# Second weight sums on GpSimd, gate store buffers moved, and alternating output banks in the last score phase of an attention and gate kernel

## The chip, the cores and the metric

One core of one Trainium2 chip. The metric is the device time of one execution in microseconds (us), as the median of a kernel's runs. Before: 920.76 us, median of 3 runs (919.71 to 922.02). "Span" is the profiled execution from its first to its last instruction; it is about 1.8 us shorter than the time of the same run.

## The reference, cut to what matters

```python
# x [1, 2048, 640]; k_cache, v_cache [1, 32, 2048, 192]; wq [640, 6144]; wo [6144, 640]
# w_gate, w_up [640, 1536]; w_down [1536, 640]; all bf16
def _A_ref(x, k_cache, v_cache, wq, wo):          # attention over the last W = 512 keys, 32 heads of 192
    q = (x @ wq) by heads
    k, v = k_cache[:, :, Sk - W:, :], v_cache[:, :, Sk - W:, :]
    p = softmax(q @ k^T * Dh ** -0.5)
    return (p @ v) by rows @ wo
def _B_ref(x, w_gate, w_up, w_down):              # gate
    return (sigmoid(x @ w_gate) * (x @ w_up)) @ w_down
# ... (setup, layernorm, silu)
xn = layernorm(x)
return x + _A_ref(xn, ...) * silu(_B_ref(xn, ...))
```

## The kernel before: the parts that matter

First comes the gate part: four stages of gate and up products, each followed by a down projection (D in the tables is the last of them). Then attention runs over 8 groups of 4 heads, each group twice (once per half of the rows), so 16 runs of a score phase (S) and an attention phase (V). The queries of the next run are worked out between the score groups, and the output products of the run before between the attention groups. The last run differs: its score phase carries the output products of run 15, and after its attention phase comes a tail with its own output products.

The query products use sums and differences of halves of the weights, so each group of heads needs a "raw" load of weights, a scaling to fp16 and a handful of sums in each of 5 chunks:

```python
    def scale_k(key):
        nc.gpsimd.tensor_scalar(k_of[key][:], k_of[key][:], w_down, None, op0=ALU.mult)
    # ...
    def scale_w(g, c):
        raw = raw_t[g, c][:]
        nc.scalar.activation(raw.bitcast(F16), raw, AF.Copy, scale=w_up)
        for k, r in enumerate((LO, HI)):
            nc.scalar.activation(sums_w(g, c, r, 0), part_w(g, c, r, k, 0), AF.Copy)

    def sum_w(g, c):
        a, tt = slice(0, P), nc.vector.tensor_tensor
        TA, TB, TC = (sums_w(g, c, a, i) for i in range(1, 4))
        tt(TB, part_w(g, c, a, 1, 1), part_w(g, c, a, 0, 1), ALU.subtract)
        tt(TA, TB, part_w(g, c, a, 0, 0), ALU.add)
        nc.scalar.activation(sums_w(g, c, HI, 2), part_w(g, c, HI, 1, 1), AF.Copy)
        tt(TC, part_w(g, c, a, 1, 0), TA, ALU.subtract)
        tt(sums_w(g, c, HI, 1), part_w(g, c, HI, 0, 1), part_w(g, c, HI, 0, 0), ALU.subtract)
```

Scores have 64 contract rows, output products have 128. An attention group ends in a transpose by DMA out of one of two output buffers:

```python
    def stage_s(r, i, pp, c, k):
        b0 = 4 + 2 * (k % 2)
        ps = ps_all[:, b0:b0 + 2, :]
        for j in range(PC):
            for b, h in enumerate((LO, HI)):                 # LO, HI: rows 0-63, 64-127
                nc.tensor.matmul(ps[:, b, :], lhsT=kT[h, ...], rhs=qT_t[r][i, j][h, pp, :], ...)
        nc.scalar.activation(E_t[r, i, pp][:, c, :, :], ps, AF.Exp, scale=scale_qk)

    def stage_pv(r, i, pp, h):
        # ... 16 matmuls, then
        nc.vector.tensor_tensor(o_st[...], o_ps[...], rden[...], ALU.mult)
        if h == 1:
            nc.sync.dma_start_transpose(oT[:], o_st[:].rearrange("p q d -> p (q d)"))
```

The first queries, and the loop over runs:

```python
    nc.scalar.activation(mx, w_up, AF.Exp, scale=0.0)        # brings the table for exponentials
    slots = query_slots(0, True, (2, 3), (4, 5), (6, 7, 0))
    for n, k in enumerate((0, 1, 7, 2, 3, 8, 4, 5, 9, 6, 10)):
        slots[k]()
        if n == 1:
            scale_w(1, 0)
        elif n == 3:
            sum_w(1, 0)
            load_raw(1, 3, nc.gpsimd)
    # ...
        for k, x in enumerate(s_list):
            stage_s(r, *x, k)
            # ... queries of the next run; in runs 0 and 1 more scale_w and sum_w
            if r == last and k % 2 == 1:
                ring[:] = [0, 1]
                stage_wo(*wo_list[k // 2])                   # one output tile: always banks 0 and 1
```

The softmax here doesn't subtract the row's maximum and nothing guards it: scores larger than these inputs give would overflow.

## Time and profile before

| what | before |
|---|---|
| median of runs | 920.76 us |
| span of the profiled run | 919.7 us |
| TensorE busy | 896.2 us, 97% |
| VectorE, ScalarE, GpSimd busy | 653.5, 446.1, 220.3 us |
| TensorE not busy | 23.5 us |

How to read it: TensorE is the bound, so a microsecond off another engine is worth nothing unless TensorE waited for it. The 23.5 us without work are the reserve that these shares show (time at a lowered clock counts as busy and comes on top), and they sit in a few stages. So the view that decides is the length of each stage beside the same stage in the steady stretch, and the waits of TensorE name who releases it there. These lines are in the prediction below.

### The profile page before, as it was taken

What the parts mean: (1) busy time and instruction counts of PE and PEld (TensorE: products, weight loads), DVE (VectorE), ACT (ScalarE), POOL (GpSimd) and SP (SyncE); (2) the same over time, 40 slices, a digit from 0 to 9 for tenths busy, and PEclk for the clock granted to TensorE, in tenths of its full rate; (3) what the DMA queues carried; (4) which work ended last, traced back from release to release, by engine and by line L of the source; (5) the groups of instructions that cost most, each with busy time, mean ns of one, the idle gap of its engine ahead of it and who ended that gap; (6) DMA issues with size and microseconds to landing.
All of it is one profiled execution on the core that took longest, in us unless ns stands there. A gap on an engine that the chain in (4) does not pass through costs nothing.

```text
span 919.7 us, 18431 instructions
## 1 busy us (share of the span) xinstructions
PE 896.2 (97%) x7706; PEld 533.6 (58%) x7785; DVE 653.5 (71%) x1089; ACT 446.1 (49%) x528; POOL 220.3 (24%) x201
## 2 busy tenths in 40 slices
PE   9999998898999999999999999999999999999987
PEld 5545454446665656666666666666666566666555
DVE  4879947568667866786678667866786678666556
ACT  4323346586428542854285428542764375424240
POOL 0052135203200320032003201320132011202962
PEclk9999999999999999999999999999999999999999
DMA  9993374407261826192617261727183624265625
GB/s 286 259 264 93 90 152 88 122 19 121 52 122 11 188 53 122 24 175 53 120 30 170 52 121 35 164 53 121 39 161 53 121 45 104 52 105 164 159 80 123
DMA packets 186612, 100.37 MB, mean 109 GB/s; under 512 B 153312, under 2 KB 178912, under 8 KB 186528
## 3 DMA queue, kind: packets, MB, share of 16 engines
q1 hardware_dynamic: 157632, 57.85, 31.4%
q0 software_dynamic: 9408, 29.93, 13.3%
q10 hardware_dynamic: 19488, 11.41, 5.5%
q8 instruction: 61, 1.00, 0.5%
q14 instruction: 23, 0.19, 0.1%
HBM read 57.87 MB, written 5.24 MB: 69 GB/s over the span
## 4 chain that ended last, share of the span: by engine, by line
PE 87%; DVE 4%; ACT 4%; DMA 3%; issue 2%; POOL 0%; SPq 0%; DVEq 0%; POOLq 0%; ACTq 0%
PE ps_all L680 21%; PE ps_all L537 19%; PE ps_all L637 17%; PE ps_all L623 16%; PE ps_all L430 8%; PE ps_all L480 4%; ACT raw L218 1%; ACT E L627 1%; DVE ps_all L694 1%; DVE o_sb L695 1%; PE ps_all L344 1%; ACT sig_sb L435 1%; DMA gB_d<-gB_sb 1%; DVE wB L225 1%; DMA oT<-o_st 1%
## 5 line engine op out<-in xcount | busy, mean ns | idle before, releaser
L627 ACT ACTIVATE E<-ps_all 128x1024 bf16<-128x1024 f32 x256 | 253.3, 1022 | 295.4 <-PE ps_all L623 224.3
L680 PE MATMUL ps_all<-wo_g,oT 128*128 128x128 bf16 (+2 forms) x1474 | 225.1, 296 | 6.4 <-DVE o_sb L695 3.1
L623 PE MATMUL ps_all<-qT,kT 64*128 64x512 bf16 x1536 | 195.3, 376 | 1.9 <-ACT E L627 1.0
L637 PE MATMUL ps_all<-v_sb,E 128*128 128x193 bf16 x2048 | 189.5, 247 | 0.1
L637 PEld LDWEIGHTS <-E 128*128 128x128 bf16 x2048 | 168.7, 98 | 18.2 <-issue 6.4
L680 PEld LDWEIGHTS <-oT 128*128 128x128 bf16 x1536 | 121.6, 98 | 82.6 <-issue 6.4
L571 DVE TENSOR_TENSOR qT<-ps_all,qp 128x512 bf16<-128x512 f32 x176 | 116.9, 688 | 51.8 <-PE ps_all L537 41.7
L558 DVE COPY qp<-ps_all 128x512 f32<-128x512 f32 x150 | 100.8, 688 | 57.8 <-PE ps_all L537 57.7
L623 PEld LDWEIGHTS <-kT 64*128 64x128 bf16 x1536 | 76.4, 94 | 90.8 <-issue 9.0
L644 DVE TENSOR_TENSOR o_st<-ps_all,rden 128x768 bf16<-128x768 f32 x128 | 122.5, 957 | 6.6 <-DMA oT<-o_st 2.0
L202 POOL DMA_DIRECT2D raw<-in_A_wq_dram x80 | 47.9, 604 | 316.5 <-ACT wB L227 235.8
L135 POOL DMA_DIRECT2D k_sb<-in_A_k_cache_dram x32 | 33.4, 1044 | 184.2 <-DMA kT<-k_sb 117.8
L142 POOL TENSOR_SCALAR k_sb<-k_sb,w_sc 128x1536 bf16<-128x1536 bf16 x16 | 67.1, 4193 | 22.2 <-DMA k_sb<-in_A_k_cache_dram 21.9
L218 ACT ACTIVATE raw<-raw,w_sc 128x1536 f16<-128x1536 bf16 x40 | 63.0, 1575 | 1.1
L480 PE MATMUL ps_all<-wd_sb,hT_sb 128*128 128x128 bf16 (+1 forms) x377 | 54.2, 303 | 2.7 <-DVE hT_sb L436 2.3
L714 DVE TENSOR_TENSOR acc<-ps_all,acc 128x640 f32<-128x640 f32 x48 | 39.6, 825 | 22.2 <-PE ps_all L680 22.2
L537 PE MATMUL ps_all<-XA,wA 64*128 64x512 f16 x420 | 52.3, 376 | 2.0 <-DVE qT L571 2.0
L643 DVE RECIPROCAL rden<-ps_all 128x4 f32<-128x4 f32 x128 | 23.2, 181 | 42.5 <-PE ps_all L637 41.2
L537 PE MATMUL ps_all<-XB,wB 64*128 64x512 f16 x420 | 52.7, 376 | 0.4 <-ACT qp L556 0.4
L537 PE MATMUL ps_all<-X,w 64*128 64x512 bf16 x420 | 52.0, 376 | 0.7 <-DVE o_st L644 0.7
L436 DVE TENSOR_TENSOR hT_sb<-ps_all,sig_sb 128x512 bf16<-128x512 f32 x48 | 32.6, 683 | 25.5 <-ACT sig_sb L435 14.8
L435 ACT ACTIVATE sig_sb<-ps_all 128x512 bf16<-128x512 f32 x48 | 28.1, 596 | 40.2 <-PE ps_all L430 37.1
(114 smaller groups left out, 768.3 us busy)
## 6 DMA issues: line engine op xcount, KB each, us to landing
raw<-in_A_wq_dram POOLq DMA_DIRECT2D x80, 192.0 KB, 3.9
k_sb<-in_A_k_cache_dram POOLq DMA_DIRECT2D x32, 192.0 KB, 4.6
wo_g<-in_A_wo_dram ACTq DMA_DIRECT2D x6, 960.0 KB, 6.8
v_sb<-in_A_v_cache_dram ACTq DMA_DIRECT2D x28, 192.0 KB, 3.8
gB_d<-gB_sb POOLq DMA_DIRECT2D x16, 160.0 KB, 2.9
gBa_sb<-gB_d SPq DMA_DIRECT2D x16, 160.0 KB, 3.8
xa_sb<-in_A_x_dram SPq DMA_DIRECT2D x16, 160.0 KB, 3.8
out_dram<-o_sb SPq DMA_DIRECT2D x15, 160.0 KB, 1.8
```

The lines of the kernel that those rows point to most:

```text
L142: nc.gpsimd.tensor_scalar(k_of[key][:], k_of[key][:], w_down, None, op0=ALU.mult)
L218: nc.scalar.activation(raw.bitcast(F16), raw, AF.Copy, scale=w_up)
L430: nc.tensor.matmul(gu[:, i, :], lhsT=w[:, c, f * P:(f + 1) * P], rhs=xnT[s][:, c, :], start=(c == 0), stop=(c == NCD - 1),)
L480: nc.tensor.matmul(oB_ps[:, d0:d0 + dsz], lhsT=hT_sb[:, f, q * P:(q + 1) * P], rhs=wd_sb[:, f, d0:d0 + dsz], start=(f == 0), stop=(f == NF ...
L537: nc.tensor.matmul(ps_all[:, b, :], lhsT=w(r, c), rhs=x[r, c, :], start=(first and k == 0), stop=(k == len(cs) - 1), skip_group_check=True,)
L558: nc.vector.tensor_copy(dst, part(b))
L571: nc.vector.tensor_tensor(q_out(i, u, pp), part(b), t[:], ALU.add)
L623: nc.tensor.matmul(ps[:, b, :], lhsT=kT[h, c * PC + j, :], rhs=qT_t[r][i, j][h, pp, :], start=(j == 0), stop=(j == PC - 1),)
L627: nc.scalar.activation(E_t[r, i, pp][:, c, :, :], ps, AF.Exp, scale=scale_qk)
L637: nc.tensor.matmul(o_ps[:, q // 2, q % 2, 0:DH + 1], lhsT=E[:, c, h, q * P:(q + 1) * P], rhs=vt[:, c, 0:DH + 1], start=(c == 0), stop=(c = ...
L644: nc.vector.tensor_tensor(o_st[:, :, h * DH:(h + 1) * DH].rearrange("p (b i) d -> p b i d", b=2), o_ps[:, :, :, 0:DH], rden[:].to_broadcas ...
L680: nc.tensor.matmul(oA[:, d0 - base:d0 - base + dsz], lhsT=oT_t[r, i, pp][:, q * PC + j, :], rhs=wo_t[runs[r][1]][:, cc, d0:d0 + dsz], star ...
```

## The change

Its intent: (1) take ScalarE and VectorE work out of the last gate stage and the first two runs by giving the second group's weight sums to GpSimd; (2) lay the buffers of the gate stores where the first queries don't write; (3) keep GpSimd's key scaling from colliding with VectorE, by moving it to VectorE; (4) give the output tiles of the last score phase two bank groups in turn; (5) cut the last output tile into three pieces.

```diff
     def scale_k(key):
-        nc.gpsimd.tensor_scalar(k_of[key][:], k_of[key][:], w_down, None, op0=ALU.mult)
+        nc.vector.tensor_scalar(k_of[key][:], k_of[key][:], w_down, None, op0=ALU.mult)
... (scale_w is split into scale_raw and copy_w; sum_w takes its engine as an argument)
+    def second_w(c):
+        copy_w(1, c, nc.gpsimd.tensor_copy)
+        sum_w(1, c, nc.gpsimd.tensor_tensor, nc.gpsimd.tensor_copy)
+        load_raw(1 + (c + 3) // NCD, (c + 3) % NCD, nc.gpsimd)
 
     with ExitStack() as bctx:
+        gpool = bctx.enter_context(tc.tile_pool(name="gpool", bufs=4))
         wB = bctx.enter_context(tc.tile_pool(name="wB", bufs=1))
         bwork = bctx.enter_context(tc.tile_pool(name="bwork", bufs=2))
-        gpool = bctx.enter_context(tc.tile_pool(name="gpool", bufs=4))
...
-                    for c in {0: (0,), 2: (1,), 5: (2,), 7: (3,), 10: (4,)}.get(f, ()):
+                    for c in {0: (0,), 2: (1,), 5: (2,), 8: (3,)}.get(f, ()):
                         scale_w(0, c)
-                    for c in {1: (0,), 3: (1,), 6: (2,), 8: (3,), 11: (4,)}.get(f, ()):
+                    for c in {1: (0,), 3: (1,), 6: (2,), 9: (3,)}.get(f, ()):
                         sum_w(0, c)
...
-                if s == 3 and q in (1, 2):
-                    sum_x(pi, 3 + q, sw)
-                elif s == 3 and q == 3:
-                    load_k((1, 0))
+                if s == 3:
+                    if q == 0:
+                        scale_w(0, NCD - 1)
+                    else:
+                        scale_raw(1, q - 1)
+                    if q == 1:
+                        sum_w(0, NCD - 1)
+                        load_raw(1, 2, nc.gpsimd)
+                    if q < 3:
+                        sum_x(pi, 3 + q, sw)
+                    else:
+                        load_k((1, 0))
...
         if r == last and i * TQ + q == 2 * TQ - 1:
-            ps, h = bank2(), D // 2
-            for e in range(2):
-                wo_mm(ps[:, e, :], r, i, q, [(e * h, h)], e * h)
-                finish(ps[:, e, 0:h], gates[t], t, e * h, (e + 1) * h)
+            cuts = [0, D // 2, D - P, D]
+            for e, (d0, d1) in enumerate(zip(cuts, cuts[1:])):
+                ps = ps_all[:, (6, 7, 2)[e], 0:d1 - d0]
+                wo_mm(ps, r, i, q, [(d0, d1 - d0)], d0)
+                finish(ps, gates[t], t, d0, d1)
...
-    slots = query_slots(0, True, (2, 3), (4, 5), (6, 7, 0))
+    slots = query_slots(0, True, (2, 3), (4, 5), (0, 1, 6))
     for n, k in enumerate((0, 1, 7, 2, 3, 8, 4, 5, 9, 6, 10)):
         slots[k]()
-        if n == 1:
-            scale_w(1, 0)
-        elif n == 3:
-            sum_w(1, 0)
-            load_raw(1, 3, nc.gpsimd)
+        if n < 3:
+            second_w(n)
...
-            if r == 0 and k == 6:
-                scale_w(1, 1)
... (the other sums of the second group go too)
+            if r == 0 and k in (7, 11):
+                scale_raw(1, 3 + k // 8)
+                second_w(3 + k // 8)
             if r == last and k % 2 == 1:
-                ring[:] = [0, 1]
+                ring[:] = [k // 2 % 2]
                 stage_wo(*wo_list[k // 2])
... (the scaling of the second keys of a group goes behind the fourth step of the attention phase)
```

More of the change, by code (lines that the diff above doesn't have):

```diff
@@ L214, in sums_w, with scale_raw, copy_act, copy_w @@
         return w_t[g][i][r, c].rearrange("p (j h e) -> p h j e", h=2, e=HF)
-    def scale_w(g, c):
+    def scale_raw(g, c):
         raw = raw_t[g, c][:]
         nc.scalar.activation(raw.bitcast(F16), raw, AF.Copy, scale=w_up)
+    def copy_act(dst, src):
+        nc.scalar.activation(dst, src, AF.Copy)
+    def copy_w(g, c, copy):
         for k, r in enumerate((LO, HI)):
-            nc.scalar.activation(sums_w(g, c, r, 0), part_w(g, c, r, k, 0), AF.Copy)
-    def sum_w(g, c):
-        a, tt = slice(0, P), nc.vector.tensor_tensor
+            copy(sums_w(g, c, r, 0), part_w(g, c, r, k, 0))
+    def scale_w(g, c):
+        scale_raw(g, c)
+        copy_w(g, c, copy_act)
+    def sum_w(g, c, tt=nc.vector.tensor_tensor, copy=copy_act):
+        a = slice(0, P)
         TA, TB, TC = (sums_w(g, c, a, i) for i in range(1, 4))
@@ L226, in sum_w @@
         tt(TA, TB, part_w(g, c, a, 0, 0), ALU.add)
-        nc.scalar.activation(sums_w(g, c, HI, 2), part_w(g, c, HI, 1, 1), AF.Copy)
+        copy(sums_w(g, c, HI, 2), part_w(g, c, HI, 1, 1))
         tt(TC, part_w(g, c, a, 1, 0), TA, ALU.subtract)
         tt(sums_w(g, c, HI, 1), part_w(g, c, HI, 0, 1), part_w(g, c, HI, 0, 0), ALU.subtract)
+    def second_w(c):
+        copy_w(1, c, nc.gpsimd.tensor_copy)
+        sum_w(1, c, nc.gpsimd.tensor_tensor, nc.gpsimd.tensor_copy)
+        load_raw(1 + (c + 3) // NCD, (c + 3) % NCD, nc.gpsimd)
     with ExitStack() as bctx:
+        gpool = bctx.enter_context(tc.tile_pool(name="gpool", bufs=4))
         wB = bctx.enter_context(tc.tile_pool(name="wB", bufs=1))
         bwork = bctx.enter_context(tc.tile_pool(name="bwork", bufs=2))
-        gpool = bctx.enter_context(tc.tile_pool(name="gpool", bufs=4))
         bone = bctx.enter_context(tc.tile_pool(name="bone", bufs=1))
@@ L413, in sum_x @@
                 tt(xb[HI], ev[HI], xb[HI], ALU.subtract)
-        sums = (4, 5, 6, 7, 9, 11), (2, 4, 7, 9)
+        sums = (4, 5, 6, 7, 9, 11), (2, 4, 7)
         folds = {(0, 9): 0, (0, 10): 1, (0, 11): 2, (2, 0): 11, (2, 1): 12, (2, 2): 13, (2, 4): 14, (2, 5): 15}
@@ L720 @@
     nc.scalar.activation(mx, w_up, AF.Exp, scale=0.0)
-    slots = query_slots(0, True, (2, 3), (4, 5), (6, 7, 0))
+    slots = query_slots(0, True, (2, 3), (4, 5), (0, 1, 6))
     for n, k in enumerate((0, 1, 7, 2, 3, 8, 4, 5, 9, 6, 10)):
         slots[k]()
-        if n == 1:
-            scale_w(1, 0)
-        elif n == 3:
-            sum_w(1, 0)
-            load_raw(1, 3, nc.gpsimd)
-    sum_at = {2: (2,), 5: (3,)}, {0: (0,), 1: (1,), 3: (2,), 4: (3,), 6: (4,)}
-    scale_at = {0: (2,), 1: (3,), 5: (4,)}, {0: (2,), 3: (3,), 4: (4,)}
+        if n < 3:
+            second_w(n)
+    sum_at = {0: (0,), 1: (1,), 3: (2,), 4: (3,), 6: (4,)}
+    scale_at = {0: (2,), 3: (3,), 4: (4,)}
     q_after = {1: (0,), 2: (1,), 3: (2,), 4: (3,), 5: (4,), 6: (5, 6), 8: (7,), 10: (8,), 12: (9,), 14: (10,)}
@@ L740 @@
                 q_list[j]()
-            if r == 0 and k == 6:
-                scale_w(1, 1)
-            elif r == 0 and k == 9:
-                sum_w(1, 1)
-                load_raw(1, 4, nc.gpsimd)
-            elif r == 1 and k == 0:
-                sum_w(1, 4)
-                load_raw(2, 2, nc.gpsimd)
+            if r == 0 and k in (7, 11):
+                scale_raw(1, 3 + k // 8)
+                second_w(3 + k // 8)
             if r == last and k % 2 == 1:
-                ring[:] = [0, 1]
+                ring[:] = [k // 2 % 2]
                 stage_wo(*wo_list[k // 2])
@@ L757 @@
         ring[:] = [0, 1, 2, 3]
-        new_t = g + 1 if pi == 0 and g + 1 < NG else None
+        new_t = g + 1 if pi == 0 and 0 < g < NG - 1 else None
         if new_t is not None:
-            if r > 0:
-                weight_tiles(new_t)
-                scale_w(new_t, 0)
-                scale_w(new_t, 1)
+            weight_tiles(new_t)
+            scale_w(new_t, 0)
+            scale_w(new_t, 1)
         elif pi == 1 and g + 1 < NG:
@@ L768 @@
             load_k((g + 1, 1))
-            scale_k((g + 1, 1))
         if r == last - 1:
@@ L781 @@
             if k == 3 and pi == 1 and g + 1 < NG:
+                scale_k((g + 1, 1))
                 turn_k((g + 1, 1))
@@ L789 @@
             if new_t is not None:
-                for c in sum_at[r > 0].get(k, ()):
+                for c in sum_at.get(k, ()):
                     sum_w(new_t, c)
-                    if r > 0 and c + 3 < NCD:
+                    if c + 3 < NCD:
                         load_raw(new_t, c + 3, nc.gpsimd)
-                for c in scale_at[r > 0].get(k, ()):
+                for c in scale_at.get(k, ()):
                     scale_w(new_t, c)
         if new_t is not None and g + 2 < NG:
-            for c in range(3 if r > 0 else 2):
+            for c in range(3):
                 load_raw(g + 2, c, nc.gpsimd)
```

## The prediction

> **What bounds the kernel now.** I read the page's busy shares first, then the table of stages (busy times over stretches that I cut at the stage boundaries), then the waits of TensorE, then the timeline of the stages that came out too long.
>
> ```profile
> span 919.7 us, 18431 instructions
> PE 896.2 (97%) x7706; PEld 533.6 (58%) x7785; DVE 653.5 (71%) x1089; ACT 446.1 (49%) x528; POOL 220.3 (24%) x201
> ```
>
> TensorE is busy 97%, so nothing but its own gaps can be won: 23.5 us, of which the start and the drain at the end keep about 8. The table of stages says where. Columns: stretch, its length, then busy time and instruction count of PE, PEld, DVE, ACT, POOL, then granted clock, DMA share, GB/s.
>
> ```profile
> 151.69:168.96 17.27, 14.83 (x97) 7.79 (x97) 10.92 (x15) 7.40 (x11) 5.01 (x9) 0.90 0.39 93
> 168.96:183.55 14.59, 12.13 (x107) 5.60 (x107) 8.06 (x15) 11.13 (x18) 3.12 (x5) 1.00 0.51 138
> 183.55:207.53 23.98, 22.68 (x204) 11.30 (x200) 16.44 (x28) 19.39 (x23) 1.19 (x2) 1.00 0.07 18
> 218.29:243.33 25.04, 22.44 (x202) 11.44 (x202) 19.14 (x34) 18.79 (x21) 6.54 (x5) 1.00 0.51 92
> 267.14:289.05 21.91, 21.91 (x204) 9.86 (x202) 14.60 (x22) 15.14 (x16) 0.00 (x0) 1.00 0.19 32
> 862.44:890.94 28.50, 25.17 (x190) 11.66 (x193) 12.43 (x15) 15.51 (x16) 26.06 (x19) 1.00 0.54 148
> ```
>
> The fifth row is a score phase in the steady state, 21.91 us, all busy: the floor. Against floors the other rows lose:
> - Last down projection of the gate part (row 1): the one before it on the timeline takes 12.95 us, so 4.3 us are lost.
> - First queries (row 2): 105 matmuls at the steady 0.108 us are 11.34 us; 3.25 us lost.
> - First score phase (row 3): 23.98 - 21.91 = 2.1 us. Second (row 4): 25.04 - 21.91 = 3.1 us.
> - Last score phase (row 6): 16 score groups of 0.647 us and 8 output tiles of 1.63 us are 23.4 us; 5.1 us lost.
> - One run with weight sums and a GpSimd key scaling together takes 46.7 us where the others take 45.71: 1.0 us.
>
> These are 18.8 us; 2% is 18.4 us.
>
> The waits of TensorE name the releasers (total, times, longest), and half-microsecond idle gaps cost about 0.28 us more than the wait itself, since ends are modelled: the last-phase step is 3.64 us, not 2.92.
>
> ```profile
> PE ps_all L680 <- DVE o_sb L695: 3.1, 7, 0.5
> PE ps_all L537 <- DVE o_st L644: 2.6, 2, 1.9
> PE ps_all L480 <- DVE hT_sb L436: 2.3, 2, 1.2
> PE ps_all L537 <- DVE qT L571: 2.0, 1, 2.0
> PE ps_all L623 <- DVE qT L571: 0.7, 1, 0.7
> ```
>
> Row 1 has more lost than its 2.3 us of waits. Microsecond by microsecond (stretch, length, PE busy, granted clock, DMA), TensorE idles and then gets half its clock for 3.4 us, which costs the missing 1.7:
>
> ```profile
> 155.00:156.00 1.00, 0.19 (x1) 1.00 0.83 88
> 156.00:157.00 1.00, 0.25 (x2) 0.96 0.96 295
> 157.00:158.00 1.00, 0.65 (x3) 0.50 0.09 15
> ...
> 159.00:160.00 1.00, 1.00 (x7) 0.50 0.00 0
> 160.00:161.00 1.00, 1.00 (x9) 0.84 0.22 37
> ```
>
> **What the Trainium skill says.**
> - "TensorE: Matmul & The Clock Gate", section "What's actually happening": the array falls to half clock after an idle window of some 3.4 us, windows running freely. The trace agrees on the length (0.50 from about 156.9 to 160.3) but fell with only some 2 us idle in the window, so less than a whole idle window is enough; the later 2 us idle at 172.6 did not do it. It depends on the phase.
> - "GPSIMD Engine Reference", section 3.1: about 2.6 cycles per element for two inputs. The trace has 128x640 fp32 adds on GpSimd at 1.40 us, which is 2.6 cycles at that page's 1.2 GHz: agrees.
> - Same page, section 8: it shares SBUF interfaces with a VectorE instruction that has two SBUF inputs. The trace agrees: the sum at 759.03 took 2.27 us instead of 0.35, under a GpSimd key scaling (4.17).
> - "VectorE: DVE Perf Modes", section "The perf-mode tier table": bf16 tensor-scalar in SBUF runs at up to 4x. No VectorE key scaling is in this trace; the 128x640 normalise takes 0.44. My estimate for 128x1536 is 0.6 (from the page) to 0.9 us (scaled from the trace).
>
> **The change part by part.** T is the end of the last down projection.
>
> *Fewer sums in the gate's last stage.* Before, ScalarE ran sigmoid and five weight chunks (1.57 + 2 x 0.52 + 0.52 us each, plus 1.4 us of waiting for VectorE) in 26 us and came late: hT 10 and 11 at about 155.8 and 157.3. After, four chunks stay, the fifth goes to the down projection, one input sum too. Replaying both queues with the trace's durations (VectorE waits for the second key load until at most 147.2, scales it, then catches up) gives hT 10 and 11 at 153.7 and 154.4; TensorE asks at 154.4 and 154.7. The wait and the half clock both go: **-4.3 us**, T = 164.65 instead of 168.96.
>
> *First queries.* Before, TensorE stopped 2.3 us at its 31st matmul: the first query add wrote where gate stores still left from (it waits for those DMA queues in the instruction order) and began at 173.86. After, those buffers lie elsewhere and that wait is gone. But ScalarE now does a 1.57 us raw scaling between the last sigmoid and the exponential's table load: T+0.8, +1.57, +1.30 table, +0.12, +0.59 copy, +0.7 VectorE add = T+5.2, and that raw chunk's load, issued only after the fifth sum at about T-3, lands about T+1.5, so about T+6. TensorE wants it at T+3.24: 2.7 to 2.9 us lost where 2.3 were. It is also long enough to throttle the clock in some phase of its window; I count 0.7. The later two small waits on ScalarE (0.5 + 0.5) go. Together **+0.5 us**.
>
> *First scores.* The new banks (0, 1, 6 instead of 6, 7, 0) take away the 0.74 us wait of the second score group, 1.0 with its tail, and leave 0.2 at the first new query. The two raw scalings move after score groups 7 and 11. There two groups and one query slot follow in 2.38 us against 1.95 of exponentials: no room for 1.57 us. Group 10 then waits for exponential 8: S7 + 0.86, exponential to 1.88, scaling to 3.48, exponential to 4.52, wanted at 3.03: 1.5 lost, and the same at group 14, against 1.0 before. **+1.2 us.**
>
> *Weight sums of the second group on GpSimd.* VectorE and ScalarE lose them in the first attention phase and second score phase. The first wait there (1.94) is part sums, part the 5 us transposes of the two output buffers: the third output pair waits until 12 instead of 13.2 us into the phase, so about 0.9 stays. The 0.66 after it goes. 3.1 becomes 1.0: **-2.1 us**. GpSimd per chunk, estimate: four sums of 384 elements at 0.9 to 1.2 us, three copies at 0.9: about 7.8, plus 1.2 for two load issues; started at T+5.2 when the stores have landed, five chunks end at T+50. First use is about T+53.
>
> *Key scaling to VectorE.* 14 of these lie in attention phases where VectorE has about 1 us free per 2.96 us step. The second one comes behind the fourth step, 11.7 us into the phase; its keys are there after 0.7 + 4.4 + 5.2, about 10.5. Hidden. GpSimd computes nothing then, so the collision at 759 goes: **-1.0 us**.
>
> *Output banks of the last score phase.* One bank pair was used for all eight tiles, each waiting for two VectorE instructions (0.83 + 0.82). Alternating gives these 5.8 us. Seven steps of 0.72: **-5.1 us**.
>
> *Last tile in three pieces.* VectorE gets six instructions instead of four; fixed cost about 0.17 each: **+0.2 us**.
>
> Sum: -4.3 + 0.5 + 1.2 - 2.1 - 1.0 - 5.1 + 0.2 = -10.6, so 910.2; I say 910.4.
>
> **Rivals.**
> - GpSimd becomes the bound at the second queries. Against: 10.3 us per chunk would still fit. For: its 16-bit scaling here runs at 2.7 ns per element, slower than its fp32 add at 2.2, and these operands are strided 16-bit pieces. At 12 us per chunk the second queries would start some 8 to 15 us late and the gain would vanish: 912 to 925.
> - VectorE waits for keys in seven attention phases. For: only 1.2 us of slack, and transposes share the queue. Each us beyond what the PSUM ring takes would cost 7 us in all: 912 to 918.
> - The ScalarE stalls that I add do not come (the loads land early, the clock stays up): 907.5.
> - The last score phase only trades its wait for one on the exponentials. Against: 1.95 us of them per 2.92 us step. It would give back 2 to 3 us.
>
> **Range and chances.** The gains of 5.1 and 4.3 are the firmest, the others are about 1 to 2 us each in either direction, and the clock's phase moves a run by 1.7; the three runs before spread 2.3. So 907 to 914.5. Faster by 2% needs under 902.3, all losses gone: 0.01. Slower by 2% needs GpSimd far too late: 0.02.
>
> **What would show it.** Right: no wait of the down projection on hT and clock 1.00 there; last score phase 23.4 us with no wait on o_sb; two waits of about 1.3 to 1.5 us on exponentials in the first scores; one wait of 2 to 3 us on the first query add; GpSimd sums near 1 us and done before the second queries; steady run period still 45.7. Wrong: a wait of TensorE on accumulators written by GpSimd, VectorE idle for key loads followed by TensorE waits, or a half clock in the first queries.

## The result, and the profile after

| | before | after |
|---|---|---|
| median of 4 runs | 921.0 us (919.71 to 922.02) | 915.46 us (913.47 to 915.81) |
| span of the profiled run | 919.7 us | 914.0 us |
| ratio, 95% | | 0.9936 (0.9917 to 0.9956) |

The ratio is the mean time of one kernel's runs over the mean of the other's of the same rounds, so it isn't quite the ratio of the medians. The gain is 5.5 us by the medians and 5.7 by the spans: the predicted direction, well within 2%, but half of the predicted 10.4, and outside the predicted range.

From the page of the kernel after, the span and the busy times of the engines:

```profile
span 914.0 us, 18466 instructions
PE 894.2 (98%) x7712; PEld 531.7 (58%) x7791; DVE 650.2 (71%) x1087; ACT 438.0 (48%) x513; POOL 178.6 (20%) x220
```

TensorE's busy time falls by 2.0 us only. It does the same work in nearly the same instructions, and half-clock time counts as busy. What moves is in the stages. The table of stages of the kernel after, columns as in the prediction: last down projection (D), first queries (Q), first scores (S0), first attention (V0), second scores (S1), last scores.

```profile
151.69:164.83 13.14, 13.04 (x96) 7.32 (x97) 9.28 (x13) 9.60 (x12) 4.27 (x8) 1.00 0.24 70
164.83:181.32 16.49, 13.98 (x108) 6.33 (x108) 7.17 (x12) 9.57 (x15) 9.00 (x13) 0.90 0.47 119
181.32:206.06 24.74, 22.42 (x203) 11.31 (x200) 14.99 (x23) 19.11 (x20) 20.60 (x30) 1.00 0.24 64
206.06:218.48 12.42, 10.84 (x129) 10.70 (x129) 6.44 (x12) 1.02 (x1) 4.67 (x7) 1.00 0.63 96
218.48:241.25 22.77, 22.25 (x201) 11.37 (x201) 16.86 (x27) 15.25 (x16) 0.00 (x0) 1.00 0.19 35
859.59:884.59 25.00, 24.79 (x190) 11.13 (x193) 12.43 (x15) 15.51 (x16) 23.89 (x18) 1.00 0.59 166
```

The waits of TensorE of the kernel after (total, times, longest) no longer name the output tiles or the down projection; three others lead:

```profile
PE ps_all L646 <- ACT E L650: 2.2, 2, 1.1
PE ps_all L560 <- ACT qp L579: 2.1, 3, 1.7
PE ps_all L646 <- DVE o_st L667: 1.8, 2, 1.6
```

Row by row against before, in us. "Steady" runs from the end of the second attention phase to the last scores; "tail" is what follows the last attention phase. The start, the second and the last attention phase are the same in both and left out. The lengths come from the timelines of TensorE in both profiled runs.

| stage | before | after | change | predicted |
|---|---|---|---|---|
| D | 17.27 | 13.14 | -4.13 | -4.3 |
| Q | 14.59 | 16.49 | +1.90 | +0.5 |
| S0 | 23.98 | 24.74 | +0.76 | +1.2 |
| V0 | 10.76 | 12.42 | +1.66 | 0 |
| S1 | 25.04 | 22.77 | -2.27 | -2.1 |
| steady | 595.30 | 594.53 | -0.77 | -1.0 |
| last S | 28.50 | 25.00 | -3.50 | -5.1 |
| tail | 18.00 | 18.65 | +0.65 | +0.2 |
| sum | | | -5.70 | -10.6 |

Three rows miss by more than a microsecond: Q, V0 and the last S.

### The profile page after: what moved, and what is told of

It reads as the page before. It is cut to its first block, busy times and chain, and to the rows that moved or that the text cites. A ratio compares the mean times of both kernels' runs of the same rounds, so it can differ in the third digit from the quotient of the medians.

```text
span 914.0 us, 18466 instructions
## 1 busy us (share of the span) xinstructions
PE 894.2 (98%) x7712; PEld 531.7 (58%) x7791; DVE 650.2 (71%) x1087; ACT 438.0 (48%) x513; POOL 178.6 (20%) x220
## 5 line engine op out<-in xcount | busy, mean ns | idle before, releaser
L738 DVE TENSOR_TENSOR acc_hi<-ps_all,acc_hi 128x640 f32<-128x640 f32 x48 | 39.3, 819 | 7.7 <-PE ps_all L703 7.7
```

Source lines behind the costliest of these rows:

```text
L738: nc.vector.tensor_tensor(acc[t][:], oA[:, 0:D], acc[t][:], ALU.add)
```

## The experiments

All edits are against the kernel after. All twelve kernels gave correct results. "A" in an expectation is my theory for the loss at hand, "B" its rival there. The three sets each ran on one chip with their own runs of the kernel before: medians 920.96, 921.38 and 921.39 us. Since sets differ in the chip, I compare a run with the kernel after by the ratios to before, or by stages.

### First queries: the raw scaling ahead of the copies, or the clock

The timeline of ScalarE and VectorE of the kernel after (start, length, engine, line, operation, out and in, count, and in brackets the idle time before and who ended it):

```profile
166.28 1.57 ACT L218 ACTIVATE raw<-raw,w_sc 128x1536 f16<-128x1536 bf16 x1 [0.65 <-DMA raw<-in_A_wq_dram]
167.87 1.28 ACT L744 ACT_TABLE_LOAD   x1
169.28 1.55 ACT L579 ACTIVATE qp<-ps_all 128x512 f32<-128x512 f32 x3
169.94 1.89 DVE L594 TENSOR_TENSOR qT<-ps_all,qp 128x512 bf16<-128x512 f32 x3 [3.45 <-ACT qp L579]
```

Read it from below: VectorE's first query add waited 3.45 us for a copy, which stood on ScalarE behind the table load, which stood behind a raw scaling, which itself waited 0.65 us for its load. TensorE ran out of banks from 168.07 to 170.69, which is 2.6 us with a single matmul in it. Then its clock was halved. Stretches of 1 us of TensorE of the kernel after (length, busy time, granted clock, DMA share, GB/s), with the lines of 1.00 left out:

```profile
169.00:170.00 1.00, 0.10 (x1) 1.00 1.31 370
...
171.00:172.00 1.00, 1.00 (x10) 0.72 0.98 175
172.00:173.00 1.00, 1.00 (x8) 0.50 0.34 106
...
174.00:175.00 1.00, 1.00 (x9) 0.57 0.00 0
```

**Raw scaling after the copies (e1_raw_late).**

```diff
-                    else:
+                    elif q < 3:
                         scale_raw(1, q - 1)
...
         slots[k]()
+        if n == 2:
+            scale_raw(1, 2)
```

> The changed kernel, with the raw scaling of the third chunk moved on ScalarE from before the exponential's table load to behind the three first query copies. Theory A (ScalarE's order makes the wait at the first queries, and that wait makes the half clock): the first queries take 12.3 to 13.0 us instead of 16.49, granted clock 1.00 in them, nothing else changes, so about 3.5 to 4 us less than the changed kernel (2 less where the other's run did not lose its clock). Rival B (the wait is for something else: the gate stores or GpSimd, or the table load alone): the stop at the 31st matmul stays at 1.5 us or more.

Measured: 910.67 us (909.87 to 911.06), ratio 0.9894 (0.9879 to 0.9908), against 0.9936 for the kernel after. The first queries took 12.58 us instead of 16.49, at full clock. The timeline of its TensorE in that place shows 30 matmuls in one piece:

```profile
167.85 3.79 PE L560 MATMUL ps_all<-XA,wA 64*128 64x512 f16 x30
```

So the wait was ScalarE's order. The half clock is gone with it here, and in the two combined kernels below that lack the wait as well; but six of the nine profiles that keep the wait have no half clock either (next experiment), so that it only followed from the wait is likely, not shown. V0 fell to 10.77 as well, which is taken up below. S1 took 23.27 with a wait of 1.1 us on o_st, so 0.5 came back there.

**Clock kept up by matmuls into an unused bank (e8_fill).** They change no result.

```diff
         slots[k]()
+        if n == 2:
+            for _ in range(10):
+                nc.tensor.matmul(ps_all[:, 7, :], lhsT=X1[0][:, 0, 0:P], rhs=X1[0][:, 1, :], start=True, stop=True)
```

> The changed kernel, with ten matmuls of 512 columns that nobody reads, into a free PSUM bank, issued where TensorE otherwise waits in the first queries (2.16 us of work in a wait of 2.6). The wait itself is left as it is. Theory A (the missing 1.7 us of the first queries are the half clock that follows the idle time): the first queries take 14.6 to 15.0 us instead of 16.49, clock 1.00. Rival B (the slow matmuls there come from something else, such as operands or PSUM shared with GpSimd): 16.4 or more, and the same slow matmuls.

Measured: 913.9 us (913.18 to 914.16), ratio 0.9928 (0.9914 to 0.9943). The first queries took 14.91 us at clock 1.00. That looks like a proof but isn't one: of the nine profiled runs with such a stop (2.6 to 3.2 us with one matmul in it, no filling), only three fell to half clock: the kernel after, and e7_stores_back and e11_raw_late_stores_back, whose stops are the longest (3.0 and 3.2). The other six showed 14.8 to 15.0 us at full clock. Here is the profile of the one that moves the scalings (below), for the same microsecond of which the kernel after had 0.50:

```profile
172.00:173.00 1.00, 1.00 (x14) 1.00 0.41 131
```

What the runs do show is that the same wait costs 1.7 us more in some runs than in others. The four runs of the kernel after fit this: 913.47 us at a mean clock of 0.999, and 915.12, 915.8 and 915.81 at 0.997. So the size of the clock loss is measured, its control is not: filling kept all four runs within 1 us, which agrees with it without settling it.

**Gate stores back to their old place (e7_stores_back), and the same together with the late raw scaling (e11_raw_late_stores_back).** What is the move of the store buffers worth by itself?

```diff
-        gpool = bctx.enter_context(tc.tile_pool(name="gpool", bufs=4))
         wB = bctx.enter_context(tc.tile_pool(name="wB", bufs=1))
         bwork = bctx.enter_context(tc.tile_pool(name="bwork", bufs=2))
+        gpool = bctx.enter_context(tc.tile_pool(name="gpool", bufs=4))
```

> The changed kernel with the gate store buffers back above the weights, so that the first query add waits for the gate stores again. Theory A (in the changed kernel ScalarE's chain ends as late as the stores land): the first queries take 16.0 to 17.2 us (14.5 to 15.7 if this run keeps its clock) against 16.49 (14.8 to 14.9): within 0.8 us, so this part of the change alone brings little or nothing. Rival B (the part brings the 2 us of the wait that it removes): 2 us longer.

Measured: 914.89 us (914.38 to 915.94), ratio 0.993 (0.9911 to 0.9949), the same as the kernel after. The first query add began at 170.31 us instead of 169.94, and Q took 16.86 us with the half clock in it. Of these 0.37 us, 0.24 are a later start of ScalarE's copies (169.52 instead of 169.28), since the raw load landed later in that run; the last gate store had landed at about 170.1. So in the changed kernel the move is worth 0.1 us or so, and nothing in the times, because the ScalarE chain hides the stores.

> As the run with the third raw scaling behind the query copies (first queries 12.58 us), but with the gate store buffers back above the weights. Theory A: now nothing hides the wait for the stores, and the first queries take 14.3 to 15.3 us (1.7 more if the clock falls). Rival B (that wait never mattered): 12.6 as without it.

Measured: 916.08 us (914.41 to 916.75), ratio 0.9936 (0.9913 to 0.9959), against 0.9894 for the late scaling with the buffers moved. Now ScalarE starts its copies at 166.92 but VectorE's add still begins at 170.37; in the instruction order it waits there for the queues of the gate stores, and the last of them lands at about 170.15. (The profile puts this wait down to a GpSimd sum that ends at 170.27. In e7_stores_back the add began at 170.31, before the same sum ended at 170.40, so it isn't the sum.) TensorE waits 2.79 us, and the half clock fell into the profiled run again (Q 17.05). So the move matters, by about 4 us with the half clock in it, but only once ScalarE is out of the way: two waits lay one above the other, and the change removed the lower one. The move also has a price. The second group's weight tiles lie in the accumulators, and these now share memory with the stores: in the kernel after, the last store lands at about 173.7 us and GpSimd's sums start at 174.02, where with the buffers back they start at 167.34.

### First scores: no room for the raw scalings

In the timeline of the kernel after, the scaling behind score group 7 (counted from 0, as in the code) pushes three exponentials back, and TensorE waits for one; the same happens again four groups later.

```profile
195.46 1.57 ACT L218 ACTIVATE raw<-raw,w_sc 128x1536 f16<-128x1536 bf16 x1
197.99 0.82 PE L646 MATMUL ps_all<-qT,kT 64*128 64x512 bf16 x6 [1.11 <-ACT E L650]
```

**Scalings at the long query slot and behind the last score group (e4_raw_moved).**

```diff
-            if r == 0 and k in (7, 11):
-                scale_raw(1, 3 + k // 8)
-                second_w(3 + k // 8)
+            if r == 0 and k == 6:
+                scale_raw(1, 3)
+                second_w(3)
...
         ring[:] = [0, 1, 2, 3]
+        if r == 0:
+            scale_raw(1, 4)
+            second_w(4)
```

> The changed kernel, with the two raw scalings of the first score phase moved: the first behind score group 6, where two query slots follow, the second behind the last score group (GpSimd's sums of the fifth chunk follow, and so does its load). Theory A (each scaling delays an exponential that a score group two later waits for): both waits of 1.11 us go, the first score phase takes 22.0 to 22.6 us instead of 24.74; GpSimd is still done before the second queries; as the load comes later too, the first attention phase falls below 12. 2 to 4 us less in all. Rival B (the scores there are slow for GpSimd's sums at the same time): the phase stays above 24 us.

Measured: 911.55 us (910.31 to 912.48), ratio 0.9906 (0.9886 to 0.9926). The first scores took 22.34 us instead of 24.74, both waits on exponentials are gone, and GpSimd is still in time for the second queries. V0 fell to 10.75 here too, and S1 grew by 0.24 to 23.01.

### First attention: a raw load beside a transpose

This stage was to stay as it was, and grew by 1.66 us. The timeline around it, in the kernel after:

```profile
210.12 1.20 POOL L202 DMA_DIRECT2D raw<-in_A_wq_dram  x2 [0.30 <-POOL acc_hi L238]
210.21 12.92 SPq L673 DMA_TRANSPOSE oT<-o_st  x4
217.47 0.96 DVE L667 TENSOR_TENSOR o_st<-ps_all,rden 128x768 bf16<-128x768 f32 x1 [4.35 <-DMA oT<-o_st]
218.48 0.82 PE L646 MATMUL ps_all<-qT,kT 64*128 64x512 bf16 x6 [1.58 <-DVE o_st L667]
```

And before:

```profile
211.67 12.93 SPq L650 DMA_TRANSPOSE oT<-o_st  x4
214.89 1.19 POOL L202 DMA_DIRECT2D raw<-in_A_wq_dram  x2 [11.10 <-ACT acc_hi L227]
216.75 0.96 DVE L644 TENSOR_TENSOR o_st<-ps_all,rden 128x768 bf16<-128x768 f32 x1 [1.12 <-DMA oT<-o_st]
```

After, GpSimd issues the last raw load of its sums 0.1 us ahead of the first output transpose. The slowest of the four transposes takes 7.2 us to land, where it took 5.0 before. VectorE waits 4.35 us for that buffer, so the banks of the attention groups come free late, and the next scores want those banks: 1.58 us of TensorE. The rival is that the two output buffers alone make this wait, whatever is loaded.

**The load written later in the program (e2_load_late), and the same on SyncE's queue (e2b_load_sync).**

```diff
     def second_w(c):
...
-        load_raw(1 + (c + 3) // NCD, (c + 3) % NCD, nc.gpsimd)
+        if c < 4:
+            load_raw(1 + (c + 3) // NCD, (c + 3) % NCD, nc.gpsimd)
... (after the attention groups of a run)
+        if r == 0:
+            load_raw(2, 2, nc.gpsimd)      # e2b_load_sync: nc.sync
```

> The changed kernel, with the last of the raw loads on GpSimd (it was issued at 210.1 us, as the first output transpose began) moved behind the first attention phase. Theory A (that load holds up the transpose, 7.2 us to landing where it was 5.0 before): the transpose lands in 5 us or less, VectorE's wait falls from 4.35 to about 2, the first attention phase returns from 12.42 to 10.8 us and the second score phase grows by at most 0.5: 1.2 to 1.6 us less. Rival B (two output buffers are too few at VectorE's new pace, whatever the load): the wait stays above 3.5 us and the phase above 12.

Measured: 914.8 us (913.89 to 915.51), ratio 0.9939 (0.9924 to 0.9954); V0 12.28, slowest transpose 7.0 us. A miss of the experiment, not of a theory: GpSimd had nothing else to do and nothing to wait for, so it issued the load at 208.51 us all the same. A later place in the program doesn't delay an idle queue. Inconclusive.

> The run with the load moved behind the phase in the text changed nothing: GpSimd issued it at 208.5 us all the same, since nothing made it wait. Here that load goes to SyncE's queue behind the output transposes of the phase. Theory A (a raw load issued at the moment of the first output transpose holds it up; in the two runs where the load came 1.9 us after it or later, the transpose landed in about 5.3): landing 5.6 us or less instead of 7.2, first attention phase 10.8 instead of 12.4, VectorE's wait about 2.3 instead of 4.2. Rival B (VectorE's pace brings the second transpose beside the first, load or no load): still about 7 and 12.3.

Here the load stands behind the transposes on the queue that issues them. The timeline of that run:

```profile
208.65 10.72 SPq L674 DMA_TRANSPOSE oT<-o_st  x4
213.71 0.96 DVE L668 TENSOR_TENSOR o_st<-ps_all,rden 128x768 bf16<-128x768 f32 x1 [2.15 <-DMA oT<-o_st]
219.61 1.45 SPq L202 DMA_DIRECT2D raw<-in_A_wq_dram  x2
```

Measured: 912.7 us (911.55 to 913.42), ratio 0.9904 (0.9884 to 0.9924). The slowest transpose takes 5.0 us again, VectorE waits 2.15 us, TensorE doesn't, V0 is 10.77 and S1 22.22. So the load at that moment was the cause. In e1_raw_late and e4_raw_moved GpSimd's chain ends later, the load leaves 1.9 us or more after the first transpose, the slowest transpose takes 5.6 and 5.3 us, and V0 is 10.77 and 10.75: the same cause from another side. It holds in every profile: where the load leaves up to 0.2 us ahead of the first transpose, the slowest takes 6.8 to 7.9 us, elsewhere 4.8 to 5.6. By which route a load slows a transpose the runs don't show.

### Last scores: 23.4 us predicted, 25.00 measured

The waits on the output tiles went, as predicted, yet a step takes 3.13 us, not 2.92. In the timeline of TensorE before, a line with a wait (12 score matmuls follow on such a tile):

```profile
867.50 1.79 PE L680 MATMUL ps_all<-wo_g,oT 128*128 128x512 bf16 x12 [0.45 <-DVE o_sb L695]
```

and after, without one:

```profile
862.73 1.47 PE L646 MATMUL ps_all<-qT,kT 64*128 64x512 bf16 x12
864.13 1.80 PE L703 MATMUL ps_all<-wo_g,oT 128*128 128x512 bf16 x12
```

From start to start the 12 score matmuls take 1.40 us and the 12 output matmuls 1.73, where they take 1.29 and 1.63 among their own kind. About 0.105 us is lost at each change between the two kinds, with no wait recorded. If that is so, more changes must cost more. (Not every change of kind costs this: attention groups and output products, both on 128 rows, alternate at 1.33 and 1.63 us and lose nothing.)

**Output tiles in two halves, one behind each score group (e9_halves).** Same work, 16 more changes.

```diff
-    def wo_mm(oA, r, i, q, d_ch, base=0):
+    def wo_mm(oA, r, i, q, d_ch, base=0, ccs=range(G * PC)):
         nn = G * PC
-        for cc in range(nn):
+        for cc in ccs:
...
-            if r == last and k % 2 == 1:
-                ring[:] = [k // 2 % 2]
-                stage_wo(*wo_list[k // 2])
+            if r == last:
+                b, x = k // 2 % 2, wo_list[k // 2]
+                half = flat(ps_all[:, 2 * b:2 * b + 2, :])
+                wo_mm(half, *x, d_chunks, 0, range(PC) if k % 2 == 0 else range(PC, G * PC))
+                if k % 2 == 1:
+                    t = row_tile(*x)
+                    if x[0] % 2 == 0:
+                        finish(half[:, 0:D], gates[t], t, 0, D)
```

The tiles are accumulated and finished as before; only the order of the matmuls differs.

> The changed kernel, with each output tile of the last score phase cut in two halves of six matmuls, one after each score group instead of one tile after each two: the same matmuls, twice as many changes between matmuls on 64 rows and on 128. Theory A (a change costs TensorE about 0.1 us, which makes 3.135 us of a step that should take 2.92): the last score phase takes 26.4 to 27.0 us instead of 25.0, with no waits. Rival B (the step is held by exponentials or by VectorE): 25.0 or less, as the finer mix gives the exponentials more room.

Measured: 915.83 us (915.51 to 917.37), ratio 0.9942 (0.9923 to 0.9962). The last score phase took 26.71 us, 1.71 more for 16 more changes: 0.107 us each, and no wait in it. (The ratio hardly moved from 0.9936: by the mean clocks three of this kernel's four runs kept theirs in the first queries, which hides up to 1.6 us.) Its timeline:

```profile
858.29 0.99 PE L703 MATMUL ps_all<-wo_g,oT 128*128 128x512 bf16 x6
859.21 0.82 PE L646 MATMUL ps_all<-qT,kT 64*128 64x512 bf16 x6
```

The Trainium skill names a possible reason, which I hadn't looked up: "TensorEngine Tiling (Array Packing)", section "Tiling Modes", says that changing the tiling mode drains TensorE. It gives no size. The runs agree that each change costs, with 0.105 to 0.107 us; that it is this drain is the page's reading, not something that a trace shows.

**One bank pair again (e6_one_bank_pair).**

```diff
-                ring[:] = [k // 2 % 2]
+                ring[:] = [0]
```

> The changed kernel with all output tiles of the last score phase on one bank pair, as before. Theory (this part alone brings the 3.5 us by which that phase got shorter): the last score phase takes 28.5 us instead of 25.0, each of seven tiles waits 0.45 us for the second VectorE instruction, the rest is as in the changed kernel: 3 to 4 us more. Rival (the phase got shorter because VectorE or GpSimd have less to do there): below 27.

Measured: 919.34 us (917.68 to 919.98), ratio 0.9974 (0.996 to 0.9988). The phase took 28.50 us, as before, and the waits are back in the list of TensorE's waits:

```profile
PE ps_all L703 <- DVE o_sb L718: 3.1, 7, 0.5
```

So alternating banks alone give 3.5 us, the largest single part after the down projection. Seven waits of 0.45 us make 3.1 of it, and 0.05 us per wait is left beyond them. The rest of a slow step, which I had taken for the tail of the wait, was the two changes.

### Steady stretch: the collision on the weight sums

**Key scaling back on GpSimd (e10_keys_gpsimd).**

```diff
-        nc.vector.tensor_scalar(k_of[key][:], k_of[key][:], w_down, None, op0=ALU.mult)
+        nc.gpsimd.tensor_scalar(k_of[key][:], k_of[key][:], w_down, None, op0=ALU.mult)
```

> The changed kernel with the key scaling back on GpSimd, 4.2 us each. Theory A (in the steady state the part brings only the one collision with a weight sum, which cost 1.0 us): the stretch from the second attention phase to the last score phase grows from 594.5 to about 595.3, or stays if the collision falls elsewhere; the second key scaling of the gate's last stage and its collision with the sums return, so the last down projection may wait again by up to 1 us. In all 0 to 2 us more. Rival B (the part costs time, as VectorE then waits for keys in seven phases): 1 to 3 us less.

VectorE's weight sums, duration in ns as minimum, median and maximum, with the key scaling on GpSimd, and then in the kernel after:

```profile
L234 DVE TENSOR_TENSOR wB<-raw x35: 348/349/2302, 131.2 to 766.3; 128x384 f16<-128x384 f16 x35
```

```profile
L234 DVE TENSOR_TENSOR wB<-raw x35: 339/348/349, 131.5 to 766.0; 128x384 f16<-128x384 f16 x35
```

Measured: 916.38 us (915.14 to 918.55), ratio 0.9947 (0.9933 to 0.9961); the interval overlaps that of the kernel after, so the stages decide. The steady stretch is 595.31 us against 594.53 after and 595.30 before; the collision is one sum of 2.30 us instead of 0.35. V0 took 13.13 instead of 12.42, with the slowest transpose at 7.9 us instead of 7.2, and D is 13.13 here and 13.14 after, so the down projection's gain doesn't come from this part.

### The remedies together

**All three remedies (e12_combined), and the same with the last tile in two pieces (e13_combined_two).** The first joins the edits of e1_raw_late, e4_raw_moved and e2b_load_sync. The second adds:

```diff
-            cuts = [0, D // 2, D - P, D]
+            cuts = [0, D // 2, D]
```

> The changed kernel with the three remedies together: the third raw scaling behind the query copies, the other two behind score group 6 and behind the score phase, the last raw load on SyncE. If they add: first queries 12.6, first scores 22.3, first attention 10.8, second scores 22.2 to 22.6, the rest as in the changed kernel, so a span of about 905.7 and a time of 907 to 908.5 us, and no half clock in the first queries.

> As the combined run, with the last tile in two pieces as before. Theory A (three pieces cost VectorE two more instructions at the very end): the stretch from the last output matmuls to the end of the span is 0.3 to 0.7 us shorter than in the combined run (18.7 to 19.2 us in the runs with three pieces, 18.0 in the kernel before). Rival B (the smaller last transfer pays for them): the same or longer.

Measured for three pieces: 907.28 us (906.9 to 907.51), ratio 0.9846 (0.9832 to 0.9859), span 905.4. By stages Q 12.58, S0 22.34, V0 10.76, S1 22.09. Beyond the start, the only waits of TensorE of 0.2 us or more are two of 0.2 on copies in the first queries. Worked out from the single runs: 3.91 (Q, from the late scaling) + 2.40 (S0) + 1.65 and 0.55 (V0 and S1, from the moved load) are 8.5 us; the spans differ by 8.6. The parts add up, so no new wait took their place.

Measured for two pieces: 906.08 us (905.91 to 906.21), ratio 0.9833 (0.9819 to 0.9846), span 904.1, tail 17.85 us instead of 18.84. This is the fastest kernel, 1.67% under before, and it beats both kernels. Its four runs lie within 0.3 us, at a mean clock of 1.0 each, where those of the kernel after spread 2.3. That fits: no stop of 2 us is left in the first queries for a half clock to follow.

The last tile in three pieces therefore costs 1.0 us in the stages and 1.2 in the medians. (The tails are single profiles: with three pieces they run from 18.28 us in e10_keys_gpsimd to 19.21 in e4_raw_moved. The medians are the firmer ground.) Of the 1.0, 0.4 us come before the end of the last VectorE instruction and 0.6 after it. In the kernel after the final VectorE instruction ends 1.49 us after the last matmul, before it was 1.18. The smaller last stores land no sooner: 1.9 us for 32 KB and 2.2 for 48 KB, against 1.7 for 80 KB. The Trainium skill, "DMA: Bandwidth & Descriptors", section "Anatomy of one DMA — SWDGE (gpsimd) path", puts a fixed cost of about 2.0 us on a transfer, next to which the bytes are little. These stores leave from another queue, but the trace agrees on the shape.

## Why the prediction was partly right

The sum of predicted parts was 10.6 us, and 5.7 arrived. No rival took over; the terms were off, as follows. One of the prediction's own signs of being wrong, a half clock in the first queries, came; so did the failure of one sign of being right, 23.4 us for the last score phase.

- **Fewer sums in the last gate stage (-4.3, measured -4.13): right** in size. No wait on hT is left and the clock is 1.00 in that stage in every profile of the changed kernel and its variants. No run undid this part alone, so the cause is read from the traces and not shown by an experiment. The floor was misread: the down projection before takes 13.05 us (112.75 to 125.80), not 12.95. And about 1.7 of the 4.13 are the half clock of the one profile before. It seems not to have struck in every run of that kernel: of its 23 runs in the three sets, the six with a mean clock of 0.999 took 919.2 to 920.2 us, the others 920.7 to 924.9.
- **First queries (+0.5, measured +1.90): mechanism right, size wrong, in part by luck.** The prediction's chain put the end of the first add at about T+6; it came at T+5.8, and the loss of 2.7 to 2.9 us was 2.6. Its terms (2.7 to 2.9, less 2.3, plus 0.7, less 1.0) give only +0.1 to +0.3. Two of them failed. "The later two small waits on ScalarE (0.5 + 0.5) go" didn't hold: two of 0.2 us stayed, as before. And "It is also long enough to throttle the clock in some phase of its window; I count 0.7" is an average, where a run pays all or nothing: 29 matmuls took 5.08 us instead of about 3.4, so 1.7. By the mean clocks it struck in three of the four runs, and it struck in three of nine profiles with such a stop, which would make 0.6 (in one of the seven where the stop is under 2.8 us). Where it didn't strike, the stage took 14.8 to 15.0 us, 0.2 to 0.4 over before.
- **First scores (+1.2, measured +0.76): right** in mechanism, two waits on exponentials at the two predicted places, 1.11 us each instead of 1.5.
- **Weight sums of the second group on GpSimd (-2.1, measured -0.61 in V0 and S1 together): the sums right, their side effect missed.** A sum takes 0.91 us and a chunk 5.6 with its copies, where I had 7.8 as an estimate (its own terms give 6.3 to 7.5); GpSimd was done at 209.8 us, the second queries began at 220.6. The rival with GpSimd as the bound fell. **The step that failed** is "so about 0.9 stays", the wait on the two output buffers: it is 2.1 us (1.58 at the end of V0, twice 0.26 in S1), where it was 1.94 before. GpSimd's early end puts its last load beside the first output transpose, which then takes 7.2 us where I had counted 5. I had worked out when the sums would end and not asked what GpSimd would issue then. Shown by e2b_load_sync: with the load elsewhere V0 and S1 together are 2.81 us shorter than before. The -2.27 and +1.66 of the table are partly one wait that moved from S1 into V0.
- **Key scaling to VectorE (-1.0, measured -0.77): right.** A scaling takes 0.62 us. VectorE does wait for keys in six attention phases of the steady stretch, 0.8 to 3.4 us each, but TensorE doesn't follow, so that rival fell too. Shown by e10_keys_gpsimd.
- **Output banks (-5.1, measured -3.50): mechanism right, size wrong.** "Seven steps of 0.72" took the whole gap between a slow step and the floor for the wait. The floor, "16 score groups of 0.647 us and 8 output tiles of 1.63", was joined from phases in which each kind runs among its own. With the 15 changes inside the phase at 0.105 us it is 25.0, and 25.00 was measured. The "0.28 us more than the wait itself, since ends are modelled" was mostly this cost. Shown by e9_halves and e6_one_bank_pair. The rival with a wait on exponentials in this phase fell: no wait is in it.
- **Last tile in three pieces (+0.2, measured +0.65 in the tail, 1.0 by e13_combined_two against e12_combined): too small.** VectorE's part came near the count (its last instruction ends 0.3 us later after the last matmul); the rest comes after that instruction, where I had counted nothing: the last store lands no sooner, 1.9 us against 1.7.

The misses: V0 1.66, last S 1.6, Q 1.4, tail 0.45; against them S0 0.4 and S1 0.2 to the better, and 0.2 each from D and the steady stretch to the worse. Together 4.9, the difference of 10.6 and 5.7.

Open: whether filling matmuls hold the clock (e8_fill agrees but one profile in a good phase would look the same), by what route the load slows a transpose, and, by experiment, which of the moves in the last gate stage took its wait away.

## What to carry to other kernels

Work that is moved to an engine with much idle time must still fit between two steps of its queue that others wait for: 1.57 us of scaling made TensorE stop for 2.6 us at one place and cost almost nothing a few instructions later. Ask of every engine that gets faster or ends earlier what it will issue next, and beside which short transfer on the critical path that falls; a later place in the program doesn't hold back an idle queue. A floor that is joined from separate phases lacks what it costs to alternate between them, and a removed wait is worth only the distance to the next releaser behind it, so undo the parts singly and in pairs.

## What the Trainium skill lacked or had wrong

- "TensorE: Matmul & The Clock Gate" ties the half clock to an idle window of some 3.4 us. Here stops of 2.6 to 3.2 us, with one matmul in each, brought it in three of nine profiled runs (in the kernel after 0.72, 0.50, 0.50 and 0.57 over four microseconds) and not in six (1.00), at a difference of 1.7 us; the page has the free-running window and a loop with many short stops, but not that a single stop shorter than the window can do it.
- "TensorEngine Tiling (Array Packing)" says that a change of mode drains TensorE, without a size: 0.105 to 0.107 us for each change between 64-row and 128-row matmuls here.
- "DMA: Bandwidth & Descriptors" has no size for what a plain load costs a transpose of the same core that runs beside it: the slowest took 7.2 us to land with a raw load issued just before it, and 5.0 without.
- "GPSIMD Engine Reference", section 3.1, gives about 2.6 cycles per element for two inputs. Sums of 384 fp16 elements took 0.91 us, which is 2.8 at that page's 1.2 GHz, so the figure also serves for strided 16-bit operands, which the page doesn't say.
